# Four instead of two B-projection units in token halves, and one gate product split off, in a fused SSM and GEGLU kernel

## Chip, cores, metric

One core of one Trainium2 chip. The metric is the device time of one execution in microseconds, median of several runs. All runs told here lie between 176.5 and 178.6 us, at a granted TensorE clock of 1.00 in every record; only fast runs (none over 1.5% above the fastest of its kernel), or single runs of unknown state where that is said, are compared. Each ratio is between runs of the same chip and the same rounds.

## The reference, cut to what matters

```python
xn = _layernorm(x)                                   # x: 1 x 2048 x 512
# A: state space model
Bu   = einsum("bld,pd->blp", xn, B_bar)              # the "B-projection", complex: two real products
h[t] = Lam_bar * h[t-1] + Bu[t]                      # scan over 2048 tokens
y    = 2 * (hseq @ Cmat.T).real + xn * Dskip
# B: GEGLU
z    = (gelu(xn @ w_gate) * (xn @ w_up)) @ w_down
return x + y + z
```

The kernel works in four blocks of 512 tokens (a block is four tiles of 128). For each block it normalizes x on VectorE, transposes it by DMA (at the start of block 0, TensorE transposes centred tiles instead), and TensorE then makes the gate/up products, the B-projection (8 units: 4 groups of states times real and imaginary part) and the output product.

## The kernel before, the parts concerned

Every operation is entered in program order into a list with its reads and writes. TensorE and the DMA queue keep this order; the order of VectorE, ScalarE and GpSimd is chosen by a list scheduler that has a duration for each operation (`S.schedule()`), so a change of a TensorE operation can move operations of other engines.

```python
def TR(b, js=range(4)):                       # DMA transposes of normalized x, one per tile
    for j in js:
        S.dma(... dma_start_transpose(XNT[b][:, :, 128*j:128*(j+1)], XN[...]) ..., writes=[XTk[b][j]])

def BU(b, halved=0):                          # B-projection, 8 units, one PSUM bank each
    ...
    def mm(c, s, bank, j0, j1):               # tiles j0..j1: 4 matmuls of 128*(j1-j0) columns
        ...
        PE(f, ..., [BBT...] + XTr(b)[j0:j1], [BANK[bank]])
    for unit_ in units[:halved]:
        mm(*unit_, 0, 2)                      # first two tiles of the first `halved` units
    for n, (c, s, bank) in enumerate(units):
        mm(c, s, bank, 2 if n < halved else 0, 4)
        ACT(... copy bank -> SS ...)
# ... cut ...
def ks(k, j, w_, first=False):                # step k of the gate/up product of tile j of block 0;
    for u in range(2):                        # w_: [0] gate, [1] up, [0, 1] both in one matmul
        GT_k(k, j, u, w_, first)              # waits for the weights w_ of step k, which land one by one
# ... cut ... the program order at the start
ks(0, 1, [0], True)
ks(0, 1, [1])
ch(*stats(0, 2)); ch(sub(2))                  # VectorE: centre tile 2
ks(1, 0, [0, 1])
cent_T(2, 0, 1, 6)                            # TensorE transposes of tile 2
cent_T(2, 1, 4, 7)
ks(1, 1, [0, 1])
# ... cut ...
load_B()                                      # DMA: B transposed from HBM, Dskip, x of block 2
LN(1, [0, 1]); LN(1, [2, 3])
TR(1)
# ... cut ...
BU(0)
CHAIN(0, 2)
H0_T()
BU(1, 2)
```

## Time and profile before

| | before |
|---|---|
| time, median of 3 runs (range) | 177.25 us (176.85 to 177.71) |
| the execution that was profiled | 177.77 us, span 176.5 us |
| TensorE busy | 97% of the span |
| TensorE, start-to-start loss between the token halves of block 1 | 0.719 us |
| last transpose of block 1's x lands | 32.92 us |

Losses are read from starts, as the prediction explains: the distance between the starts of two matmuls, less the pace of the first, 0.109 us for 256 columns and 0.216 for 512. A few matmul records are missing in some traces; these show as a distance of exactly one more matmul and are not waits. Landing times are those at which a transfer's semaphore reaches its full count in the trace.

### The profile page before, as it was taken

What the parts mean: (1) busy time and instruction counts of PE and PEld (TensorE: products, weight loads), DVE (VectorE), ACT (ScalarE), POOL (GpSimd) and SP (SyncE); (2) the same over time, 40 slices, a digit from 0 to 9 for tenths busy, and PEclk for the clock granted to TensorE, in tenths of its full rate; (3) what the DMA queues carried; (4) which work ended last, traced back from release to release, by engine and by line L of the source; (5) the groups of instructions that cost most, each with busy time, mean ns of one, the idle gap of its engine ahead of it and who ended that gap; (6) DMA issues with size and microseconds to landing.
All of it is one profiled execution on the core that took longest, in us unless ns stands there. A gap on an engine that the chain in (4) does not pass through costs nothing.

```text
span 176.5 us, 2485 instructions
## 1 busy us (share of the span) xinstructions
PE 172.0 (97%) x866; PEld 83.9 (48%) x881; DVE 159.8 (91%) x278; ACT 95.0 (54%) x187; POOL 9.8 (6%) x24
## 2 busy tenths in 40 slices
PE   8899999899999999999999999999999999999995
PEld 3545564544644444444644444444464444444454
DVE  6886999995999999879999999999999999999941
ACT  5464768799876899265676693000657970000000
POOL 3122040202000000000100000000000000000000
DMA  5899999895899000001134000002001000000312
GB/s 152 222 332 174 240 146 194 142 134 105 177 263 295 0 4 2 0 30 59 33 61 89 0 0 0 4 0 87 32 0 30 4 0 0 0 0 0 119 63 61
DMA packets 32420, 14.36 MB, mean 81 GB/s; under 512 B 23736, under 2 KB 32408, under 8 KB 32408
## 3 DMA queue, kind: packets, MB, share of 16 engines
q1 hardware_dynamic: 32240, 14.07, 36.7%
q8 instruction: 7, 0.11, 0.3%
q10 hardware_dynamic: 168, 0.13, 0.2%
q14 instruction: 5, 0.04, 0.1%
HBM read 6.46 MB, written 2.10 MB: 48 GB/s over the span
## 4 chain that ended last, share of the span: by engine, by line
PE 80%; DVE 6%; DMA 6%; SPq 4%; issue 2%; POOL 1%; DVEq 0%; POOLq 0%
PE PS L884 37%; PE PS L843 29%; PE PS L749 11%; DMA arena<-arena 6%; PE PS L817 2%; SPq L484 2%; DVE arena L599 1%; DVE arena L610 1%; SPq L489 1%; DVE arena L597 1%; DVE arena L629 1%; DVE arena L724 1%; SPq L493 1%; POOL arena L552 1%; DVE arena L864 0%
## 5 line engine op out<-in xcount | busy, mean ns | idle before, releaser
L884 PE MATMUL PS<-arena 128*128 128x512 bf16 (+3 forms) x317 | 65.9, 366 | 0.3
L843 PE MATMUL PS<-arena 128*128 128x512 bf16 x257 | 57.1, 379 | 0.4
L884 PEld LDWEIGHTS PS<-arena 128*128 128x128 bf16 (+1 forms) x323 | 30.8, 98 | 35.2
L843 PEld LDWEIGHTS PS<-arena 128*128 128x128 bf16 x264 | 25.8, 98 | 30.2
L787 DVE TENSOR_TENSOR_SCAN arena<-arena 128x512 bf16<-128x512 f32 x32 | 38.8, 1254 | 0.0
L858 ACT ACTIVATE arena<-PS 128x512 bf16<-128x512 f32 x33 | 19.8, 599 | 24.8 <-DVE arena L902 16.7
L749 PE MATMUL PS<-arena 128*128 128x512 bf16 (+1 forms) x134 | 28.2, 366 | 0.7 <-DMA arena<-arena 0.6
L862 ACT ACTIVATE arena<-PS 128x512 bf16<-128x512 f32 x33 | 19.8, 601 | 4.7 <-PE PS L843 4.7
L749 PEld LDWEIGHTS PS<-arena 128*128 128x128 bf16 x136 | 13.2, 98 | 14.9 <-DMA arena<-arena 0.8
L876 ACT ACTIVATE PS<-arena 128x512 f32<-128x512 bf16 (+2 forms) x17 | 9.6, 581 | 19.7 <-DVE arena L902 19.0
L758 ACT ACTIVATE arena<-PS 128x512 bf16<-128x512 f32 x32 | 17.6, 594 | 2.5 <-PE PS L749 2.5
L902 DVE TENSOR_TENSOR arena<-PS,arena 128x512 bf16<-128x512 f32 (+2 forms) x17 | 10.8, 652 | 6.3 <-PE PS L884 6.3
L864 DVE TENSOR_TENSOR arena<-arena 128x512 bf16<-128x512 bf16 x33 | 13.2, 417 | 2.2 <-ACT arena L862 2.0
L776 DVE TENSOR_TENSOR arena<-arena 128x4096 bf16<-128x4096 bf16 (+1 forms) x5 | 9.2, 1859 | 0.8 <-ACT arena L606 0.8
L774 DVE TENSOR_TENSOR arena<-arena 128x4096 bf16<-128x4096 bf16 (+1 forms) x5 | 9.2, 1859 | 0.3 <-ACT arena L605 0.3
L799 DVE TENSOR_TENSOR arena<-arena 128x4096 bf16<-128x4096 bf16 x4 | 9.1, 2287 | 0.1
L800 DVE TENSOR_TENSOR arena<-arena 128x4096 bf16<-128x4096 bf16 x4 | 9.1, 2283 | 0.0
L610 DVE BATCH_NORM_STATS2 arena<-arena 128x6 f32<-128x512 bf16 x12 | 7.7, 678 | 0.5 <-DMA arena<-in_A_x_dram 0.5
L721 ACT ACTIVATE arena<-PS,arena 128x256 bf16<-128x256 f32 (+1 forms) x16 | 6.1, 446 | 2.5 <-DVE arena L556 1.6
L712 PE MATMUL PS<-arena 128*128 128x512 bf16 (+1 forms) x40 | 7.1, 336 | 0.0
L724 DVE SCALAR_TENSOR_TENSOR arena<-PS,arena 128x256 bf16<-128x256 f32 (+1 forms) x16 | 6.3, 444 | 0.6 <-PE PS L701 0.6
L701 PE MATMUL PS<-arena 128*128 128x512 bf16 (+1 forms) x28 | 6.0, 348 | 0.4 <-issue 0.4
(95 smaller groups left out, 123.6 us busy)
## 6 DMA issues: line engine op xcount, KB each, us to landing
out_dram<-arena SPq DMA_DIRECT2D x15, 128.0 KB, 1.7
arena<-in_A_x_dram SPq DMA_DIRECT2D x3, 512.0 KB, 5.9
arena<-in_B_w_down_dram SPq DMA_DIRECT2D x1, 1280.0 KB, 7.0
arena<-in_B_w_gate_dram SPq DMA_DIRECT2D x4, 128.0 KB, 3.1
arena<-in_B_w_up_dram SPq DMA_DIRECT2D x4, 128.0 KB, 3.4
arena<-in_B_w_gate_dram SPq DMA_DIRECT2D x1, 480.0 KB, 6.9
arena<-in_B_w_up_dram SPq DMA_DIRECT2D x1, 480.0 KB, 7.8
arena<-arena SPq DMA_TRANSPOSE x25, 3.1
```

The source lines that it names most:

```text
L610: return (V(lambda e: e.bn_stats(ST[tt].ap, X[tt].ap), d_dve_1x(512), [X[tt]], [ST[tt]], "bnst"), V(lambda e: e.bn_aggr(MVt[b][j].ap, ST[t ...
L749: ins_ = e.matmul(PS[bank][:, 128 * j0:128 * j1], BBT[c][dk].ap[:, 128 * s:128 * (s + 1)], XNT[b].ap[:, dk, 128 * j0:128 * j1], start=(dk ...
L758: GATE["evBu"] = ACT(lambda e, bank=bank, k3=k3, s=s, c=c: e.activation(SSc[k3][s][c].ap, PS[bank][:, :], ACTF.Copy), d_act(512), [BANK[ba ...
L774: V(lambda e, s0=s0, s1=s1: e.tensor_tensor(TA.ap[:, s0:s1], ssb.ap[:, s0:s1], cos4[:, s0:s1], ALU.mult), d_dve_tt2x(1024 * step), [ss, CO ...
L787: V(lambda e, g=g, rb=rb, init=init: e.tensor_tensor_scan(g.ap, rb, g.ap, init, ALU.mult, ALU.add), d_dve_scan(512), [g, PA[RRr]] + ([CARc ...
L843: ins_ = e.matmul(PS[bank][0:m, c0:c1], W.ap[:, dk, 128 * ft:128 * ft + m], XNT[b].ap[:, dk, c0:c1], start=(dk == 0), stop=(dk == KD - 1))
L858: GATE["last_gelu"] = ACT(lambda e, bg=bg, kk=kk, m=m: e.activation(GG[kk].ap[0:m, :], PS[bg][0:m, :], ACTF.Gelu_apprx_tanh), d_act(512), ...
L862: ACT(lambda e, bu=bu, kk=kk, m=m: e.activation(UPB[kk].ap[0:m, :], PS[bu][0:m, :], ACTF.Copy), d_act(512), [BANK[bu]], [UPB[kk]], "evU")
L864: V(lambda e, kk=kk, m=m, ft=ft, k2=k2: e.tensor_tensor(HTt[k2][ft].ap[0:m, :], GG[kk].ap[0:m, :], UPB[kk].ap[0:m, :], ALU.mult), d_dve_tt ...
L876: ACT(lambda e: e.activation(PS[bank][:, c0:c1], X[tt].ap[:, c0:c1], ACTF.Copy), d_act(c1 - c0), [X[tt]], [BANK[bank]], "seed")
L884: ins_ = e.matmul(PS[bank][:, c0:c1], l_[:, 128 * j:128 * (j + 1)], r_[:, c0:c1], start=False, stop=last and n == len(ops) - 1, skip_group ...
L902: V(lambda e: e.tensor_tensor(OUTB[ko].ap[:, c0:c1], PS[bank][:, c0:c1], XD[tt].ap[:, c0:c1], ALU.add), d_dve_1x(c1 - c0), [BANK[bank], XD ...
```

## The change

It means to fill two idle places of TensorE. With four units in halves there is twice the work on the first two tiles of block 1 before TensorE needs the last two; and the gate product of step 1 of tile 0 no longer waits for the up weights.

```diff
-        ks(1, 0, [0, 1])
+        ks(1, 0, [0])
+        ks(1, 0, [1])
@@
-        BU(1, 2)
+        BU(1, 4)
```

## The prediction

> **What bounds the kernel now.** I read the page's busy shares first, then the chain of waits, then TensorE in order of time around the two places the change touches, then the waits of the other engines.
>
> The page of the kernel before:
>
> ```profile
> PE 172.0 (97%) x866; PEld 83.9 (48%) x881; DVE 159.8 (91%) x278; ACT 95.0 (54%) x187; POOL 9.8 (6%) x24
> ```
>
> TensorE (PE) is busy 97% of a 176.5 us span. The chain that ended last, in order of time (start, length, what):
>
> ```profile
> 29.17 3.75 DMA arena<-arena
> 32.92 0.14 issue
> 33.06 3.62 PE PS L749 x20
> ...
> 162.05 12.54 PE PS L884 x76
> 174.59 0.02 issue
> 174.62 0.29 DVE arena L902
> ```
>
> From 33.06 us to the last output the chain is PE with no wait: I listed every start-to-start distance of matmuls from 33 to 175 us, and all larger than one matmul's pace are about 0.43 us (or 0.30 after a 192-column matmul), which is one record missing. So a microsecond taken out of PE before 33.06 comes out of the end, if the feeding engines keep up. The same stretches of PE in the timeline (start, length, ..., idle before and releaser):
>
> ```profile
> 5.33 0.60 PE L701 MATMUL PS<-arena 128*128 128x256 bf16 x4
> 6.38 0.59 PE L701 MATMUL PS<-arena 128*128 128x512 bf16 x2 [0.45 <-issue]
> ...
> 24.56 7.94 PE L749 MATMUL PS<-arena 128*128 128x512 bf16 x39
> 33.06 3.19 PE L749 MATMUL PS<-arena 128*128 128x256 bf16 x18 [0.56 <-DMA arena<-arena]
> ```
>
> Only these two idle stretches exist after the warm-up. The first is the matmul of step 1 of tile 0 that the change splits; the second sits between the first and second token halves of the two halved B-projection units of block 1. It waits for the last transposes of the normalized x of block 1, on the DMA queue:
>
> ```profile
> 24.89 5.55 SPq L736 DMA_TRANSPOSE arena<-arena  x4
> ```
>
> The four are issued at 24.89, 26.13, 27.45 and 29.17, and land at 30.86, 31.36, 32.35 and 32.92.
>
> **What the Trainium skill says.** "TensorE: Matmul & The Clock Gate", section "Back-to-back issue gap", gives a warm spacing of N/2.4 + 2.5 ns: 109.2 ns for 256 columns, 215.8 for 512. The trace agrees: the halved units' matmuls start at 31.469, 31.578, 31.687, 31.796 (0.109 apart), full ones 0.216 apart. So a halved unit costs 8 x 0.109 = 0.872 us against 4 x 0.216 = 0.864. Its weight loads double, but a load lasts 98 ns in this trace and fits under a 109 ns matmul. "Perfetto Trace Analysis", section "Tensor Engine Instruction (MATMUL, LD_WEIGHTS)", says that the end of a matmul is estimated, not observed. The trace agrees: a 256-column matmul is recorded as about 270 ns while its successor starts 109 ns after it. So I take gaps from starts: the true loss at the second place is not the 0.56 shown. The last first-half matmul starts at 32.233, the next could start at 32.342 and starts at 33.061: **0.719 us lost**. At the first place the last matmul starts at 5.655, the next could at 5.764 and starts at 6.376: 0.612 lost.
>
> **Part 1, four units halved.** Removed: 8 matmuls of 512 columns in two units. Added: 16 of 256 columns in their place, 8 more weight loads. Moved: 8 of the 16 go ahead of the wait, as they read only the tokens that landed by 31.36.
> - Work ahead of the wait grows by 8 x 0.109 = 0.872 us, more than the 0.719 lost. The first halves of four units begin at 31.469 and end at 31.469 + 16 x 0.109 = 33.21.
> - The last transpose lands at 32.92 and its matmul could start at 33.06. It would now start at 33.21: the wait is covered with 0.15 us to spare.
> - Cost of the smaller matmuls: 16 x 0.109 - 8 x 0.216 = 0.016 us.
> - Net: 0.719 - 0.016 = **0.70 us** less on PE.
>
> Are the four banks free? Units of block 1 reuse the banks of block 0's units, whose ScalarE copies are:
>
> ```profile
> 26.03 1.09 ACT L758 ACTIVATE arena<-PS 128x512 bf16<-128x512 f32 x2
> 27.35 0.60 ACT L758 ACTIVATE arena<-PS 128x512 bf16<-128x512 f32 x1 [0.22 <-PE PS L749]
> 28.22 0.60 ACT L758 ACTIVATE arena<-PS 128x512 bf16<-128x512 f32 x1 [0.27 <-PE PS L749]
> ```
>
> Units 0 to 3 are out by 28.82, the third first half is wanted at 31.469 + 8 x 0.109 = 32.34. No wait.
>
> **Part 2, gate half by itself.** Two 512-column matmuls become four of 256: +0.004 us. The gate weights of step 1 land at 5.43, the up weights at 6.28; the evacuated transpose is ready at 5.48. So the gate half runs at 5.764 to 5.98, in the idle time, and the up half still starts at about 6.376 but takes 0.218 instead of 0.432. PE is 0.21 us early at 6.59. I do not expect it to last:
> - to 17.5 us PE stays early by most of it: the up weights of step 3 land at 9.12 (wanted at 9.40), those of the second column range at 12.49 (wanted at 12.65);
> - block 0's B-projection starts at 24.562 and needs the transposed B, which lands at 24.42; a landing costs 0.06 to 0.14 us until the matmul, so it cannot start before some 24.48;
> - block 1's first halves need the transpose that lands at 31.36. The kernel before starts them at 31.469, 0.11 after it: already as early as this landing permits.
>
> So what is left of part 2 by 31.47 us is 0.00 to 0.02 us. Could it speed the transposes themselves? VectorE feeds them, and it is not held by PE:
>
> ```profile
> 16.92 0.16 DVE L553 TENSOR_TENSOR arena<-arena 128x4 f32<-128x4 bf16 x1 [1.46 <-POOL arena L552]
> ```
>
> It stands still for 1.46 us for a GpSimd power that needs a parameter transpose landing at 15.66, so anything earlier ahead of 15.46 is lost in this wait; after it VectorE works without a pause until the normalizations of 24.45 to 26.43.
>
> **Sum.** 0.70 + 0.00 to 0.02 = 0.7 us; 177.25 - 0.70 = **176.55 us**.
>
> **Will the rest follow 0.7 us earlier?** The tightest places after 33 us:
> - The gate/up products of block 1 take the PSUM banks in a ring of four pairs; the fifth tile starts on PE at about 45.6 and needs the gate of the first out, 43.03 + 0.60 = 43.63: slack 2.0 us, 1.3 after the shift. ScalarE is full from 33.70 to there, but its first copy moves from 33.70 to about 33.84 only, and units 2 and 3 are then there earlier.
> - Block 0's output product adds its states at 64.61 + 44 x 0.216 = 74.1 us, and needs the scaled C, made on VectorE by 69.67 + 2.73 = 72.40: slack 1.7, 1.0 after.
> - The last block's states are ready at 162.25 (last line of its chain: 161.03 + 1.22); PE reaches them after 76 matmuls of block 2 and 33 of block 3 from 141.69, at 141.69 + 109 x 0.216 = 165.2: slack 3.0, 2.3 after.
>
> None turns into a wait by 0.7 us.
>
> **Rivals.**
> 1. *The wait is only pushed along, or hidden anyway.* If VectorE (91% busy) set the end, 0.7 us on PE would be given back and the time stay at 177.2. For it: the share, and the chain before 29 us, which is largely VectorE. Against it: after 33 us PE waits for nobody, and the slacks above.
> 2. *The transposes land later.* The first of the four takes 5.97 us from issue to landing, because a 512 KB load of x (lands 30.29) is ahead of it; later, alone, such a transpose takes 2.5. The DMA share there is near full. If the last landed at 33.3 instead of 32.92, 0.2 us of wait would come back: 176.75. But the kernel before would suffer the same, so this moves the result less than it seems.
> 3. *The order of instructions changes.* The kernel orders ScalarE, VectorE and GpSimd by a list scheduler over all operations; splitting three may flip neighbours anywhere. It could lift the power's wait of 1.46 us off VectorE (the waiting evacuations run first), bring the transposes and part 2 forward, and give up to 1 us more: 175.6. Or it could delay a sine table or a scan so that one of the slacks breaks: 177.5 to 178. I cannot see this from the profile of before; it is most of my range.
> 4. *Part 2 carries through.* Its 0.2 us would give 176.35. The 31.36 landing speaks against it.
>
> **Range and chances.** The three runs of before spread from 176.85 to 177.71, so the median of a few runs moves by about 0.3 us. With rival 3 at about 0.5 us either way, I take 175.9 to 177.2. A change of 2% is 3.5 us, five times the whole loss at the second place; only a bad reordering could do that upwards.
>
> **What would show it.** In the changed kernel's profile: PE on the B-projection line continuous from 24.5 to 38.1 us with 32 matmuls of 256 columns on it instead of 16, and no idle time for a DMA at 33; block 1's gate product starting 0.7 earlier than 38.9; four 256-column matmuls around 5.8 to 6.6 and the idle 0.45 cut by half; block 1's first halves still at 31.4 to 31.5 us. The prediction is wrong if the normalizations of block 1 or their landings move by more than 0.2 us, if PE shows a new wait after 33 us, or if the order of ScalarE's sine tables and copies differs.

## The result, and the profile after

| | before | after |
|---|---|---|
| median of 6 runs (range) | 177.26 us (176.85 to 177.71) | 177.22 us (176.90 to 177.45) |
| ratio after / before | | 0.9994 (0.9975 to 1.0012) |
| profiled execution, span | 177.77 us, 176.5 | 176.90 us, 175.6 |

A ratio here is the mean time of one kernel's fast runs over that of the other's of the same rounds, so not quite the ratio of the medians; the bracket is its 95% interval. The two profiles alone would have said 0.9 us faster.

The page and the chain of the changed kernel (start, length, what):

```profile
PE 171.9 (98%) x876; PEld 84.9 (48%) x891; DVE 160.0 (91%) x278; ACT 95.2 (54%) x187; POOL 11.9 (7%) x24
```

```profile
6.08 0.36 DVE arena L950
6.44 0.05 issue
6.49 0.40 PE PS L679 x4
6.88 2.83 PE PS L701 x13
...
26.66 8.19 PE PS L749 x53
34.85 0.05 issue
34.90 3.40 PE PS L749 x15
...
161.08 12.54 PE PS L884 x76
173.62 0.02 issue
173.65 0.29 DVE arena L902
```

Now the chain is TensorE from 6.49 us to the end: no DMA is left at 33 us. TensorE in order of time at the two places, in the changed kernel:

```profile
5.30 1.04 PE L701 MATMUL PS<-arena 128*128 128x256 bf16 x8
6.49 0.40 PE L679 MATMUL PS<-arena 128*128 128x128 bf16 x4 [0.15 <-DVE arena L950]
...
24.29 14.02 PE L749 MATMUL PS<-arena 128*128 128x512 bf16 x78
38.14 5.34 PE L843 MATMUL PS<-arena 128*128 128x512 bf16 x24
```

The wait of 0.719 us at 33 us is gone, as foretold. At the first place TensorE no longer waits for the up weights, but then it waits for VectorE to centre tile 2, 0.31 us from start to start. And two things in the same trace say that the halves were not what removed the wait at 33 us. The DMA queue of the changed kernel:

```profile
22.96 0.43 SPq L478 DMA_DIRECT2D arena<-in_A_x_dram  x1
23.90 5.30 SPq L736 DMA_TRANSPOSE arena<-arena  x4
30.82 1.19 SPq L829 DMA_TRANSPOSE arena<-arena  x1
```

The transposes are issued from 23.90 us, not 24.89, and the last lands at 31.37, not 32.92. The first halves begin at 31.19, so with two halved units TensorE would have wanted it at 31.19 + 0.87 = 32.06: there was nothing to wait for even without the change. And the up weights of step 1 landed at 5.77 in this execution, 6.28 in the other, with the same load instructions before them.

Part of the earlier transposes is the change's own. Comparing the instruction lists, part 1 (not part 2) made the scheduler reorder VectorE, ScalarE and GpSimd near block 1's normalization:

```
VectorE, old: stats, stats, sbq, aggr, aggr, sbq, hmul, k1, rq, norm, norm, hmul, rq, norm, norm
VectorE, new: sbq, stats, stats, aggr, aggr, rq, sbq, norm, norm, hmul, hmul, rq, norm, norm, k1
ScalarE, old: copy, copy, copy, cosine table      new: cosine table, copy, copy, copy
```

So three theories. **A**: the 0.72 us wait was that one execution's late landing; in the ordinary execution of before there is little to remove. **B**: the wait is in every execution, and the new order of the other engines gives the gain back. **C**: TensorE got a new wait elsewhere that the changed kernel's one good execution does not show.

### The profile page after: what moved, and what is told of

Its sections match the earlier page's. It is cut to its first block, busy times and chain, and to the rows that moved or that the text cites. A ratio compares the mean times of both kernels' runs of the same rounds, so it can differ in the third digit from the quotient of the medians.

```text
span 175.6 us, 2504 instructions
## 1 busy us (share of the span) xinstructions
PE 171.9 (98%) x876; PEld 84.9 (48%) x891; DVE 160.0 (91%) x278; ACT 95.2 (54%) x187; POOL 11.9 (7%) x24
## 4 chain that ended last, share of the span: by engine, by line
PE 95%; DMA 2%; DVE 1%; SPq 1%; issue 1%
PE PS L884 37%; PE PS L843 32%; PE PS L749 16%; PE PS L712 4%; PE PS L817 3%; PE PS L701 2%; DMA arena<-in_A_x_dram 2%; SPq L484 0%; DVE arena L610 0%; PE PS L679 0%; SPq L493 0%; DVE arena L950 0%; DVE arena L902 0%; DVE arena L611 0%
## 5 line engine op out<-in xcount | busy, mean ns | idle before, releaser
L843 PEld LDWEIGHTS PS<-arena 128*128 128x128 bf16 x264 | 25.7, 98 | 30.3
L749 PE MATMUL PS<-arena 128*128 128x512 bf16 (+1 forms) x142 | 28.0, 355 | 0.1
L749 PEld LDWEIGHTS PS<-arena 128*128 128x128 bf16 x144 | 14.1, 98 | 13.4
L712 PE MATMUL PS<-arena 128*128 128x512 bf16 (+1 forms) x40 | 7.1, 336 | 0.0
L817 PE MATMUL PS<-arena 128*128 128x192 bf16 x64 | 5.9, 246 | 0.0
```

The costliest lines, as they stand in the source:

```text
L712: ins_ = e.matmul(dst, XCd(j, k), WGU[:, :, k, f0:f1], start=(k == 0), stop=(k == KD - 1))
L749: ins_ = e.matmul(PS[bank][:, 128 * j0:128 * j1], BBT[c][dk].ap[:, 128 * s:128 * (s + 1)], XNT[b].ap[:, dk, 128 * j0:128 * j1], start=(dk ...
L817: ins_ = e.matmul(dst, XNT[b].ap[:, dk, 128 * j:128 * (j + 1)], WGU[:, :, dk, f0:f0 + m], start=(dk == 0), stop=(dk == KD - 1))
L843: ins_ = e.matmul(PS[bank][0:m, c0:c1], W.ap[:, dk, 128 * ft:128 * ft + m], XNT[b].ap[:, dk, c0:c1], start=(dk == 0), stop=(dk == KD - 1))
```

## Experiments

The orders of the three scheduled engines can be fixed independently of TensorE's work, since both kernels have the same operations on them:

```diff
         S.schedule()
+        made = {e: [o for o in S.ops if o.eng == e] for e in ENGINES}
+        S.order.update({e: [made[e][i] for i in idx] for e, idx in OLD_ORDER.items()})
         S.emit()
```

(In the first two kernels only the stretches that differ were exchanged, to the same effect.) All waits are derived from the data after this, so nothing is taken away; each such kernel gave a correct result, as did all others that ran.

**1. The changed TensorE work in the old order.** Edit: the diff of the change, and the order pinned to that of before.

> The changed kernel's TensorE work (both parts), with VectorE, ScalarE and GpSimd in the order of the kernel before. Theory A (the 0.72 us wait of the profiled run of before was mostly that one execution's late landing; in the median execution little of it is there): ratio to before 0.997 to 1.000, time about 177.0 to 177.25. Theory B (the wait is in every execution, and the new order of VectorE and ScalarE gives the gain back): ratio 0.996 or lower, about 176.55. Theory C (the change moves the wait elsewhere on TensorE): ratio near 1, and the profile shows a new wait of 0.5 us or more after 24 us. Under A the profile shows TensorE continuous from 24.5 to 38 us.

Measured: 177.25 us (6 runs), ratio 1.0009 (0.9991 to 1.0027). No wait on TensorE after 24 us. B would have gained 0.7 us here, and C would have shown a wait: neither. The last transpose landed at 31.65 us, although the order is that of before.

**2. The TensorE work of before in the new order.** Edit: the kernel before, pinned to the order of the changed one.

> The TensorE work of before (two halved units, step 1 of tile 0 whole), with the other engines in the order that the changed kernel has. Theory A: ratio 0.997 to 1.001, and the transposes of block 1 land by themselves some 0.5 us or more earlier than in the old order, because the normalizations come ahead of a table step; no wait at 32 us, or one under 0.2. Theory B (the new order costs what the halves gain): ratio 1.003 or more, about 177.9.

Measured: 177.39 us, ratio 1.0017 (0.9999 to 1.0036). The 0.7 us loss that B asks for (1.004) is outside the interval; a cost of some tenths is not excluded, but its profile has no wait after 7 us and its late point is the start (the up weights of step 1 land at 6.59). The last transpose landed at 30.77.

**3. Part 2 alone**, with the order unchanged by it. Edit: only the first hunk of the diff.

> Part 2 alone; the order of all other engines is unchanged by it. Theory A: ratio 0.998 to 1.001; the profile has two halved units in the old order, so it is another sample of the wait at 32 to 33 us: shorter than 0.72 us from start to start (0.0 to 0.5) if that one was an unlucky execution. Theories B and C: again 0.6 to 0.8 us.

Measured: 176.91 us, ratio 0.9995 (0.9976 to 1.0013). Two halved units, old order, and no wait at 32 us: the last transpose landed at 31.72.

**4. No unit halved.** Edit: `BU(1)` in the old order. The first try did not build (my pinning assumed that the scheduler's result had the same stretch to be replaced); the second is the same experiment.

> No unit of block 1 halved, old order everywhere: TensorE wants the last transpose at about 31.5 us instead of 32.3. If the last transpose lands at 32.9 in every execution (theories B, C), TensorE loses 0.87 us more than before: ratio 1.005, about 178.1. If it lands mostly at 31.5 to 32.2 (theory A), it loses 0.1 to 0.7 more: ratio 1.0005 to 1.004, and the profile shows a landing before 32.5.

> Mends the pinning of no_halves_old_order; expectation unchanged. No unit of block 1 halved, old order on all other engines: TensorE wants the last transpose of block 1 at about 31.4 us. If it lands at 32.9 in every execution: ratio 1.005, about 178.0, and a wait of 1.5 us in the profile. If it lands at 31.4 to 31.9 as in the two profiles of the old order just taken (theory A): a wait of 0.1 to 0.6 us there and a ratio of 1.001 to 1.003.

Measured: 177.72 us (177.31 to 178.56), ratio 1.0029 (1.0010 to 1.0047), that is 0.5 us (0.2 to 0.8 by the interval). The profile has a wait of 0.283 us at 31.77, after a landing at 31.53. So halving two units, as before already did, is worth about 0.5 us; had the last landing been at 32.9 as a rule, it would have been worth 0.87.

**5. The kernel before, three more profiles.**

> The kernel before, unchanged, once more with a profile: what is its wait between the token halves of block 1 in an ordinary execution? Theory A: the last transpose lands between 31.3 and 32.2 us and the wait is under 0.1 us from start to start in at least two of the three copies; the shown 0.72 was one execution's. Theories B and C: 0.6 to 0.8 us in all three.

> As before_again_1. In each copy the last matmul should start 166.8 to 166.9 us after the first transpose of tile 2, plus whatever the wait at 32 to 33 us is.

> As before_again_1: under theory A a wait under 0.1 us between the token halves in at least two of the three copies; under B and C 0.6 to 0.8 us in all.

Measured: 177.26, 177.05 and 177.13 us (single runs of unknown state, beside a median of 177.25 of before on that chip). TensorE around block 1, one fence for each copy:

```profile
24.80 11.41 PE L749 MATMUL PS<-arena 128*128 128x512 bf16 x60
```

```profile
24.51 11.84 PE L749 MATMUL PS<-arena 128*128 128x512 bf16 x62
```

```profile
24.44 11.84 PE L749 MATMUL PS<-arena 128*128 128x512 bf16 x62
```

The B-projections are one unbroken group, where the first profile had two with an idle time between. The losses between the halves are 0.000, 0.000 and 0.001 us:

| profile of before | transposes issued from | last lands | wanted at | lost |
|---|---|---|---|---|
| the one predicted from | 24.89 | 32.92 | 32.34 | 0.719 |
| again 1 | 24.75 | 31.79 | 32.58 | 0.000 |
| again 2 | 24.32 | 31.30 | 32.29 | 0.000 |
| again 3 | 24.55 | 31.97 | 32.22 | 0.001 |

("Wanted at" is the last first-half matmul's start plus 0.109.) The record does not name the chip of the first profile; was the late landing the rule there? The times say no, by an estimate: with their waits taken off, the nine profiled executions of kernels with before's TensorE order at the start took 176.93 to 177.44 us, so a wait of 0.72 in every execution would make 177.65 to 178.16; five of the six runs of before beside the changed kernel took 176.85 to 177.56. This settles it for A. The issue times differ by half a microsecond, the landings by 1.6. The lateness can be followed back along the queue: in the late one the B transposes landed at 24.42 and 26.06, against 23.0 and 24.6 in copy 1, the 512 KB load of x after them at 30.29 against 28.88, and then the four transposes. Why the B transposes landed late stays open.

**6. The late landing made on purpose.** If A is right, the halves should work where the landing is late in every execution. Edit, in two kernels with the old order, `BU(1, 2)` and `BU(1, 4)`: a load that nobody reads, into memory that is unused until later, between the second and the third transpose of block 1.

```diff
-        TR(1)
+        TR(1, [0, 1])
+        S.dma(lambda e: e.dma_start(dum.ap, x2[0:512, :]...), 512 * 1024, writes=[dum])
+        TR(1, [2, 3])
```

> The kernel before with its order, and the landing made late on purpose: a 512 KB load that nobody reads is put on the DMA queue between the second and the third transpose of block 1. Theory A says that with a late landing the wait of the profile of before comes back, in every execution: last landing at about 33 us or later, a wait from start to start of 0.7 to 1.5 us, ratio 1.004 to 1.008. If the load is hidden the wait is under 0.3 and this pair tells nothing.

> The same late landing with four halved units. Theory A, and the prediction's own step: the wait is shorter by 8 x 0.109 = 0.87 us than in late_halves2, down to zero, and the ratio lower by the same 0.004 to 0.005 (about 0.8 us). If halving does not shift the wait as worked out, the two are equal.

Measured: two halves 178.35 us, ratio 1.0049 (1.0035 to 1.0063); four halves 177.84, ratio 1.0021 (0.9996 to 1.0046). TensorE with two halves, then with four:

```profile
24.32 7.94 PE L749 MATMUL PS<-arena 128*128 128x512 bf16 x39
33.50 2.76 PE L749 MATMUL PS<-arena 128*128 128x256 bf16 x16 [1.23 <-DMA arena<-arena]
```

```profile
24.60 11.64 PE L749 MATMUL PS<-arena 128*128 128x512 bf16 x67
```

With two halves the shape of the first profile is back (landing 33.36, 1.395 us lost from start to start); with four it is gone (landing 32.94, second halves from 33.26). With two halves that second execution would have wanted its operand at 33.26 - 0.87 = 32.39, and lost some 0.7 us (an estimate from these starts, and the 0.14 us from landing to matmul). In the times the difference is 0.0028, 0.5 us; I expected 0.8. With four runs each the two intervals overlap, so the times alone do not show a gain; that the wait goes is shown by one profile of each. One of the four runs with four halves took 178.53, as long as those with two; it has no profile, so whether its landing was later still stays open.

**7. Part 1 alone**, in the order that it brings. Edit: only the second hunk.

> Part 1 alone, with the new order that it brings. Theory A: ratio 0.998 to 1.002 and no wait at 32 to 33 us; TensorE's pass through step 1 of tile 0 as in before, 0.53 us from the landing of its up weights to the transposes of tile 2, where the changed kernel has 0.31. Prediction's reading: 0.996.

Measured: 177.05 us, ratio 0.9999 (0.9983 to 1.0014). No wait at 32 to 33 us; last landing 30.28.

**8. Another order of the start.** What does set the time, if not the wait? In every profile TensorE runs unbroken from the second part of block 0's gate/up products (line 712) to the end, but for the wait between the halves. From the start of the first matmul of line 712 to that of the last matmul of all:

| | from line 712 to the last matmul | lost between the halves | first matmul of line 712 at |
|---|---|---|---|
| before, again 1, 2, 3 | 162.51, 162.51, 162.51 us | 0.00 | 11.38, 11.09, 11.01 |
| before, first profile | 163.22 | 0.719 | 11.14 |
| after, and again later | 162.53, 162.53 | 0.00 | 10.86, 11.36 |
| late landing, two halves | 163.90 | 1.395 | 10.89 |
| late landing, four halves | 162.53 | 0.00 | 11.18 |

To 0.03 us the last matmul starts at "when line 712 starts, plus 162.5, plus the wait". From there to the end of the span it is another 2.06 to 2.29 us; this scatter was not followed up. Ahead of the last matmul, then, the only other thing to gain is at the start. Edit, with four halves and the old order: the gate halves of step 1 of both tiles, which do not need the up weights, go first, and the up halves after the transposes of tile 2.

```diff
-        ks(1, 0, [0, 1])
+        ks(1, 0, [0])
+        ks(1, 1, [0])
         cent_T(2, 0, 1, 6)
         cent_T(2, 1, 4, 7)
-        ks(1, 1, [0, 1])
+        ks(1, 0, [1])
+        ks(1, 1, [1])
```

> Old order, four halves, and in step 1 the gate halves of tiles 0 and 1 first, then the transposes of tile 2, then the two up halves, so that the landing of the up weights (5.8 to 6.6 us in the profiles so far) is wanted only at 6.7. If the end follows from when TensorE passes this place (in all five profiles the last matmul starts 166.8 to 166.9 us after the transposes of tile 2, less the wait at 33), it gains 0.1 to 0.5 us over before: ratio 0.997 to 0.9995, last matmul start at 173.1 to 173.4. If the time of the start does not matter, ratio 1.000.

Measured on the first chip: 177.04 us, ratio 0.9974 (0.9959 to 0.9989), faster than before. It did not hold. The same with two halves, on a second chip:

> both_gates_then_ups with two halved units as in before: is its gain (ratio 0.9974) of the start alone? If so the ratio is again 0.996 to 0.999 and the profile shows no wait at 32 to 33 us. If the four halves carried part of it, the ratio is 0.999 or more, or the profile has a wait of some tenths there. It starts block 1's second halves up to 0.3 us earlier than before does, so a wait of 0.0 to 0.2 us is possible where the last transpose lands after 31.9.

Measured: 177.27 us, ratio 1.0013 (0.9994 to 1.0031), with 0.150 us lost between the halves (landing 32.29). To tell the chip from the halves, both, and the changed kernel, on a third chip:

> The same kernel on another chip, beside its two-halves twin and the changed kernel. If the gain of 0.26% is the start's own: ratio 0.996 to 0.999 again. If it was that chip's landings: 0.999 to 1.001.

> If the four halves carry the gain, this is 0.001 to 0.003 (0.2 to 0.5 us) slower than both_gates_then_ups_b in the same call, and its profile has a wait at 32 to 33 us. If the chip made the difference, the two agree within 0.0015 (0.3 us).

> The changed kernel itself on this chip: ratio 0.998 to 1.001 as on the first one (0.9994). A further profile of its start: the transposes of tile 2 at 6.4 to 6.8 us, and no wait at 32 to 33 us.

Measured: 1.0003 (0.9989 to 1.0018), 1.0004 (0.9987 to 1.0021), and 0.9998 (0.9982 to 1.0014) for the changed kernel. All the same as before; the two agree with each other, although the one with two halves lost 0.182 us between its halves in the profile. So there is no version here that beats both kernels, and the 0.26% belonged to one chip's runs. On that chip before had its highest median, 177.43 us (177.10 to 177.26 in the other sets); experiments 4 and 6 are measured against the same runs, so their ratios may be some 0.001 too small. The starts of two of these executions show what varies there. First the new start, then the changed kernel:

```profile
5.33 1.19 PE L701 MATMUL PS<-arena 128*128 128x256 bf16 x8
6.93 0.40 PE L679 MATMUL PS<-arena 128*128 128x128 bf16 x4 [0.40 <-DVE arena L950]
```

```profile
5.83 1.36 PE L701 MATMUL PS<-arena 128*128 128x256 bf16 x8
7.02 0.39 PE L679 MATMUL PS<-arena 128*128 128x128 bf16 x4
```

In the first, the x of tile 2 came late, VectorE centred it late (its statistics begin at 5.57 after a wait for the load, against 5.13 in the profile of before), and TensorE's transposes waited for that. In the second, TensorE waited for nobody: its 256-column matmuls start 0.213 us apart until 6.5 us, half pace, and 0.109 apart after that. In the profile of before the up weights were last. Three different things end the start, in turns.

## Why the prediction was wrong, step by step

It said 176.55 us, 175.9 to 177.2; measured were 177.22, and 177.13 on a later chip.

- **What bounds the kernel: right.** TensorE without a wait after the token halves of block 1 in every profile; no slack that I listed turned into a wait.
- **The cost of smaller matmuls: right.** 0.016 us worked out; 162.53 against 162.51 us measured.
- **What four halves cover: right in kind.** With the landing made late, the profiled wait of 1.395 us becomes none (one profile of each, the second with a landing 0.4 us earlier). In the times 0.5 us of the expected 0.8, with intervals that overlap.
- **"0.719 us lost", the term of the sum: wrong. This is the step that failed.** I took the loss of one execution for the loss of each. In three more executions of the same kernel it is 0.00; the mean of the five profiles with before's own order, two halves and before's loads (the four above and the one of part 2 alone, 0.001) is 0.14 us. An average gain of 0.14 - 0.02 us is within what the ratios 0.9994, 0.9998 and 0.9999 allow; it cannot be told from zero by them.
- **The warning was on the table.** The profiled execution took 177.77 us, longer than all three timed ones, and 0.52 above their median, nearly the size of the wait that I then read out of it. Of 61 timed runs of before over all experiments, on five chips or more, 3 took 177.7 us or more.
- **Rival 2 was dismissed by a wrong argument.** I wrote that a later landing would hurt the kernel before as well. The question was the other way round: how often before meets a late landing at all. Rival 1 ("hidden anyway") had the right time, 177.2, for the wrong reason: VectorE did not set the end. No rival said that the wait might be missing from the ordinary execution.
- **Part 2: small, but not for the reason given.** I held that the landing at 31.36 of the second transpose would swallow the gain. In the other profiles that landing is at 28.2 to 30.6, and the first halves of the changed kernel began at 31.19 and 31.69, with nothing to wait for. Part 2 saves some 0.2 us in executions in which the up weights are last at the start (0.27 us from their landing to the transposes of tile 2 in the profile of experiment 1, 0.53 in that of before); in others the x of tile 2 or the pace of TensorE is. In the mean nothing is seen (ratio 0.9995 with an interval of 0.0018 either way).
- **Rival 3 came true and did not matter.** The order changed, and the landings moved by more than 0.2 us: two of the prediction's own signs of being wrong, in a profile that also had its main sign of being right, no wait at 33 us. The last transpose lands at 30.25 to 31.37 us in the four profiles with the new order, at 31.26 to 32.92 in the eleven with the old order and no added load: some 1.2 us earlier in the mean. But it is hardly ever wanted that early, and 1. and 2. exclude a cost or gain of 0.7 us.

What stays open: how often the late landing comes (one of five profiles); whether the new order costs some tenths (experiment 2: 1.0017, with an interval that just reaches 1); and how late the landing was in the slow run with four halves.

## What to carry to other kernels

A profile is one execution: before you subtract a wait that ends with a DMA landing, compare the profiled execution's own time with the median, and profile the same kernel two or three times more to see whether the wait is there each time. Where one engine runs unbroken from some point to the end, write the time as "start of that stretch plus its constant length plus waits"; it shows in one line what a change can gain and what is scatter. A gain of 0.3% seen on one chip wants a second chip before it is believed.

## What the Trainium skill lacked or had wrong

- "TensorE: Matmul & The Clock Gate", section "What's actually happening", has, in one sentence, the point at which TensorE reaches full pace vary by 500 ns either way. Here, with the same warm-up matmuls, profiles show full pace from about 3.7 us (third copy of before: 128-column matmuls 0.060 us apart) to about 6.5 us (changed kernel, last run): a range of 2.8 us, and in the latter the transposes of tile 2 start at 7.02 us with nothing waited for.
- The same page, section "Back-to-back issue gap", gives about 131 ns per matmul for sustained 512-column matmuls with their weight loads. Here such pairs keep 216 ns over 162 us; the formula N/2.4 + 2.5 ns, which the section gives for an isolated matmul, holds for 512 and 256 columns (109 ns).
- The same page, section "LDWEIGHTS (loading the stationary operand)", gives columns / 1.2 ns, 107 for 128 columns; recorded are 95 to 99 ns.
- No page that I read says how much the landing of one and the same DMA moves from execution to execution. Here the last transpose of block 1 landed at 31.26 to 32.92 us in eleven profiles with the same order of issue (on several chips), and the up weights of step 1 at 5.69 to 6.59 us in the profiles told here.
